# A routing step moved by one chunk, mixed rows copied by DMA and turned in one pass, and two zero products fewer

## The chip, the cores and the metric

The kernel runs on one core of one Trainium2 chip. The metric is the time of one execution on the device, in microseconds. The engines are named as the profile names them: PE is TensorE (PEld its weight loads), DVE is VectorE, ACT is ScalarE, POOL is GpSimd, and SP is SyncE, which here only issues DMAs.

## What is computed

Three layers stand behind one another, all in float32 at the interface.

1. Attention with a window of 64 keys: 4 batches, 8 heads, 576 positions, 64 per head.
2. A mixture of experts over the 2304 rows of 512 that come out. Each row goes to the two of 8 experts whose noisy logits are highest, and the two results are added with softmax weights:

```python
noisy_logits = x @ w_gate + np.log1p(np.exp(x @ w_noise)) * noise
top2 = np.argpartition(-noisy_logits, 2, axis=1)[:, :2]
h = np.maximum(x[mask] @ w1[e], 0.0)
out[mask] += top2_w[mask, k, None] * (h @ w2[e])
```

3. A dense layer of 2048 hidden values with a gate that is quadratic between -1 and 1:

```python
h = x @ w_in
g = np.where(h >= 1, h, np.where(h <= -1, 0.0, (h + 1) ** 2 / 4))
out = g @ w_out
```

## The kernel before

**Attention and routing.** `step(u)` runs the attention of 18 tiles of 128 rows, two steps per tile. Ahead of it PE works through zero products (`warm(9)`, L662), whose result nobody uses, and then forms the first scores (`A`, L347). Beside the attention the rows' logits are formed (`Gm`), and the generator `route(g)` (L490) turns the logits of a group of tiles into expert numbers and positions; there are three groups, of 8, 4 and 6 tiles. A generator is taken on by one or more of its `yield`s each time `advance` (L636) is called. For the last group the order in which it does so is: the gate's logarithm on DVE and ACT; the noise; the two largest with their indices (L529 to L533); the one-hot sum `ohs` (L543) and counts; the position products on PE (L558 to L564), which read `ohs`; the positions on DVE (L567 to L581). After that `mark_r` and `mark_e` make one-hot marks on DVE and ACT, and `place` (L628) multiplies them on PE, so that lists of row numbers per expert come out.

The last group is not finished when the attention ends. `tail` (L796) takes it on, and `more()` (L1278) takes `tail` on by one call. In the loop over `seq` (L1288) the first unit, `ui == 0`, has eight chunks; in each, `more()` is called before the next chunk's first product (L1307) and after it (L1349), and for chunk 0 once more after its second product (L1365).

**Experts.** A unit is a set of up to 704 gathered rows of one expert. A chunk is 128 of its hidden values: `mm1` (L877, L891) makes the first product, ACT applies ReLU and writes a rounded high part (L899), DVE writes the rest (L902), and `mm2` (L948, L964) adds up the second product. All products are three single-pass products of high and low parts (type `fp32r`). Iteration `s` of the loop issues `mm1` of chunk `s + 1`, then `mm2` of chunk `s`. Every engine works through its instructions in the order in which the program issues them, and waits for others by semaphores. Between the products, weights of the next unit are split into high and low parts (`split_w`, `split_out`). Results are scattered by POOL's indirect DMAs to `y_dram`, which holds for every row its two experts' results.

**Dense groups.** The last layer runs over five groups of 2, 4, 4, 4 and 4 blocks of 128 rows. For each block:

- `prep_gather` (L1015) loads the two results of its rows, `y1` and `y2`, into the scratch pool `sc` (for the second group's blocks 0 to 2 into one tile of `raw`). SP issues these loads, for the second group POOL.
- The mix `w1*y1 + w2*y2` is made in one of two ways. `prep_mix` (L1039; first group and groups three to five) scales both on ACT and adds them on POOL. `mix_two` (L1032; second group) scales `y1` on ACT and does the rest on DVE in one operation (L1036).
- The mixed block is turned by four transposes against an identity: `xpose` (L751, L759) for the first group, `xturn` (L1230, L1236) for the others. Rows that were gathered for the experts have type `F32R` and are turned against `idr`; mixed rows are float32 and are turned against `idn`.
- ACT copies the turned block out of the bank (L762, or `xcopy`, L1242).

For the first group, block `b` is loaded in chunk `3 + b` of the last expert unit, mixed at the head of the next chunk (before that chunk's `mm1`), and turned ahead of `mm2` of the chunk after that. For the second group, `FILL` (L1402) says in which first product of the first group a block is mixed, and `TURN` and `COPY` (L1397) at which pair of chunks and which seventh `(p, j)` it is turned and copied. Groups three to five are loaded, mixed and turned in pairs 0 to 3 of the group before (L1437 to L1446). From the second group on the first product is a seven-product scheme on half blocks (`wino`, L1178), with the gate on ACT and DVE (L1196 to L1206).

Of the kernel before, what the change touches and what calls it, by code (L numbers as in the profile page):

```python
# [11 lines left out]
F32 = mybir.dt.float32  # L12
F32R = mybir.dt.float32r
# [4 lines left out]
AF = mybir.ActivationFunctionType  # L18
ALU = mybir.AluOpType
AX = mybir.AxisListType  # L20

P = 128
B, H, S, D = 4, 8, 576, 64
N = B * S
DM = H * D
# [32 lines left out]
def fused_kernel(ctx, tc, qT, kT, v, wg, noise, wcat, out, wd=None):  # L58
# [595 lines left out]
    def warm(n, to=OB[:, 1, :]):  # L654
        for _ in range(n):
            nc.tensor.matmul(to, lhsT=wz[:, 0:P], rhs=wz, start=True, stop=True)
# [2 lines left out]
        nc.tensor.matmul(IDS[:, 0:2 * NK], lhsT=wz[:, 0:P], rhs=wz[:, 0:2 * NK], start=True, stop=False)  # L659

    open_ids()
    warm(9)  # L662
    A(0)
    for u in range(2):
        top(u)
# [68 lines left out]
            gat["0a", b] = t  # L734


    xT = {}
    WD, WX = NB * P, CAPS[0]
    TR = bank[7]
# [11 lines left out]
    def xpose(key, b, m=P, TR=TR):  # L751
        if key not in xT:
            xT[key] = x_tiles(key, F32R)
        hi, lo = xT[key]
        t = gat.pop((key, b))

        o, i = (TR.bitcast(F32R), idr) if t.dtype == F32R else (TR, idn)
        for k in range(4):
            nc.tensor.transpose(o[:, k * P:k * P + m], t[0:m, k * P:k * P + P], i[0:m, 0:m])  # L759
        tv = TR.rearrange("p (k t) -> p k t", k=4)[:, :, 0:m]  # L760
        sl = slice(b * P, b * P + m)
        nc.scalar.activation(hi[:, :, sl], tv, AF.Copy)  # L762
        nc.vector.tensor_tensor(out=lo[:, :, sl], in0=tv, in1=hi[:, :, sl].bitcast(F32), op=ALU.subtract)
# [267 lines left out]

    def mix_two(un, b):  # L1032
        (y1, y2), t = gat[un["key"], b]
        nc.scalar.activation(y1, y1, AF.Copy, scale=wts[:, t, 0:1])
        yield
        nc.vector.scalar_tensor_tensor(out=y2, in0=y2, scalar=wts[:, t, 1:2], in1=y1, op0=ALU.mult, op1=ALU.add)  # L1036
        gat[un["key"], b] = y2

    def prep_mix(un, b):  # L1039
        if un["e"] is None:  # L1040
            y, t = gat[un["key"], b]
            y1, y2 = y
            nc.scalar.activation(y1, y1, AF.Copy, scale=wts[:, t, 0:1])
            nc.scalar.activation(y2, y2, AF.Copy, scale=wts[:, t, 1:2])  # L1044
            nc.gpsimd.tensor_tensor(out=y2, in0=y2, in1=y1, op=ALU.add)  # L1045
            gat[un["key"], b] = y2

    def prep_xpose(un, b, tr=TR):
        xpose(un["key"], b, n_rows(un, b), tr)
# [180 lines left out]
    def xturn(ui, b):  # L1230
        un = units[ui]
        t = gat.pop((un["key"], b))
        free = [bank[7]] + [x for x in bank[2:7] if x not in units[ui - 1]["m2"]]
        held[ui, b] = to = free[b % len(free)]
        for k in range(4):
            nc.tensor.transpose(to[:, k * P:k * P + P], t[:, k * P:k * P + P], idn)  # L1236

    def xcopy(ui, b):
        if b == 0:
# [38 lines left out]
    def more(k=1):  # L1278
        for _ in range(k):
            next(rest, None)  # L1280
# [7 lines left out]
    for s in range(len(seq)):  # L1288
# [15 lines left out]
            dec_load(ndl)  # L1304
            ndl += 1
        if ui == 0:
            more()  # L1307
        if s == NF:
            choice_weights()
        if ui == U7A - 1 and f == 2:  # L1310
# [22 lines left out]
                    prep_xpose(x, b, bank[0] if ui == WIDE else bank[4] if ui == WIDE - 1 and b == NB else TR)  # L1333
        for x, b, w in ahead:
            if f == w + 1 and x["e"] is None:
                fill.append(lambda x=x, b=b: prep_mix(x, b))
        while fill:
            fill.popleft()()

        while ndone < min(s + 2, len(seq)):  # L1340
            do_mm1(ndone)
            ndone += 1
        if decode and ndec < n64:
            dec_a(ndec)
        if s == len(seq) - 1:
# [15 lines left out]
        do_mm2(s, ahead_xpose)  # L1361
        if s in (0, 2):
            rest_w(EW - 2 + s // 2, slice(0, 1024))
        if s == 0:
            more()  # L1365
        for _ in range(SPLITS[ui][f] if ui in SPLITS else int(0 < ui < U7A)):

            if nsplit == SP:
# [20 lines left out]
        if ui == U7B and f:  # L1389
# [4 lines left out]

    AT = ({(4, 0): (None,), (4, 4): (0,), (4, 5): (1,), (5, 0): (2,), (5, 1): (3,), (5, 3): (4,), (6, 2): (5,), (6, 3): (6,)},
          {})
    TURN, COPY = {(3, 0): (0,), (3, 1): (1,), (3, 6): (2,), (4, 0): (3,)}, {(3, 3): (0, 1), (4, 2): (2, 3)}  # L1397
    g1 = FIRST2 + 1

    def later(fn, *a):  # L1400
# [9 lines left out]
    for q, (ui, p) in enumerate(items):  # L1410
# [22 lines left out]
        for j in range(7):  # L1433
            if nxt:
                late = ui == FIRST2
                if late:
                    if p == 0 and j < 4:  # L1437
                        prep_gather(nxt, j)
                elif p < 2 and j in (0, 1):
                    prep_gather(nxt, 2 * p + j)  # L1440
                if not late:
                    if 1 <= p < 3 and j in (2, 4):
                        prep_mix(nxt, 2 * (p - 1) + j // 2 - 1)
                    if 2 <= p < 4 and j in (1, 3):
                        xturn(ui + 1, 2 * (p - 2) + j // 2)
                        xcopy(ui + 1, 2 * (p - 2) + j // 2)  # L1446
                else:
                    for b in TURN.get((p, j), ()):
                        xturn(ui + 1, b)
                    for b in COPY.get((p, j), ()):  # L1450
                        xcopy(ui + 1, b)
                    if p == 4 and j > 4:
                        xsums(ui + 1, (0, 1) if j == 5 else (2, 3))
                for x in AT[late].get((p, j), ()):
                    xsums(ui + 1) if x is None else xsplit(ui + 1, x)
            if j < len(g):
                g[j]()
            if gen:
                next(gen)
                if q == NPR - 2:  # L1460
                    close_gate()
            for x in ms[len(ms) * j // 7:len(ms) * (j + 1) // 7]:
                x()
# [33 lines left out]
```

## Time and profile before

| | us |
|---|---|
| median of 3 runs | 954.12 |
| lowest and highest | 953.84, 954.31 |
| the profiled execution | 953.95 |
| its span, first to last instruction | 952.2 |

| engine | busy us | share of the span |
|---|---|---|
| PEld | 832.8 | 87% |
| DVE | 659.5 | 69% |
| ACT | 444.3 | 47% |
| POOL | 222.1 | 23% |

Times in the profile's rows count from the span's start. An instruction of a timeline is shown with its start, its length, its engine, its line, what it writes and reads, and how many like it were merged. A bracket gives how long the engine stood idle before it and what ended that. A matmul's length holds its latency, so that matmuls that follow each other overlap; the step from one start to the next says what one costs.

### The profile page before, as it was taken

How to read it: one execution, taken by the hardware profiler on the slowest of the kernel's cores; microseconds unless marked ns; L12 is line 12 of the kernel's file. 1: busy time of each engine (PE TensorE's matmuls, PEld its weight loads, DVE VectorE, ACT ScalarE, POOL GpSimd, SP SyncE). 2: the span in 40 equal slices, each digit the busy share in tenths (PEclk: the TensorE clock that was granted, in tenths of full speed). 3: DMA queues.
4: the chain of work that ended last, by engine and by line, in shares of the span. 5: the costliest groups of instructions: out<-in, count | busy, mean ns of one | idle time of the engine just before them, and what ended most of it. 6: DMA issues, size and time to landing. Idle time of an engine off the chain costs nothing. (4 is left out here: it accounts for less than half of the span.)

```text
span 952.2 us, 18037 instructions
## 1 busy us (share of the span) xinstructions
PE 938.4 (99%) x6779; PEld 832.8 (87%) x6781; DVE 659.5 (69%) x1386; ACT 444.3 (47%) x920; POOL 222.1 (23%) x273
## 2 busy tenths in 40 slices
PE   9999899999999999999999999999999999999998
PEld 6887788988889889889888889988998899899997
DVE  5688665477997968889543377766766777677664
ACT  7897325345565555555432366343334334442221
POOL 4222013133544353354402030013002201300000
PEclk9999999999999999999999999999999999999999
DMA  8884126555888777767626567775586458556521
GB/s 269 289 271 150 50 89 195 187 194 198 285 287 285 256 233 278 258 211 250 244 89 202 201 212 254 256 235 175 177 273 208 149 173 306 174 176 207 188 94 44
DMA packets 91274, 196.95 MB, mean 207 GB/s; under 512 B 7320, under 2 KB 18072, under 8 KB 91184
## 3 DMA queue, kind: packets, MB, share of 16 engines
q1 hardware_dynamic: 83152, 171.68, 54.4%
q0 software_dynamic: 6736, 21.86, 6.4%
q10 hardware_dynamic: 1296, 2.23, 0.6%
q8 instruction: 54, 0.88, 0.4%
q14 instruction: 36, 0.29, 0.1%
HBM read 155.45 MB, written 40.29 MB: 206 GB/s over the span
## 5 line engine op out<-in xcount | busy, mean ns | idle before, releaser
L964 PE MATMUL bank<-wo,hall 128*128 128x512 f32 x864 | 237.6, 394 | 0.0
L964 PE MATMUL bank<-w,hall 128*128 128x512 f32 (+3 forms) x944 | 236.2, 398 | 0.1
L964 PEld LDWEIGHTS bank<-w,hall 128*128 128x128 f32 (+3 forms) x944 | 168.8, 185 | 35.5 <-issue 0.3
L964 PEld LDWEIGHTS bank<-wo,hall 128*128 128x128 f32 x864 | 146.7, 188 | 17.4 <-DVE hall L910 0.2
L899 ACT ACTIVATE hall<-bank 128x288 fp32r<-128x288 f32 (+6 forms) x128 | 54.0, 422 | 219.7 <-PE bank L891 197.3
L891 PE MATMUL bank<-xhie,w 128*128 128x288 f32 (+4 forms) x768 | 122.6, 302 | 0.5 <-DVE hall L902 0.4
L891 PEld LDWEIGHTS bank<-xhie,w 128*128 128x128 f32 x768 | 113.5, 188 | 7.5 <-DVE hall L902 1.3
L902 DVE SCALAR_TENSOR_TENSOR hall<-bank,hall 128x288 fp32r<-128x288 f32 (+7 forms) x168 | 59.9, 390 | 84.3 <-ACT hall L899 76.2
L149 DVE TENSOR_TENSOR w<-raw,w 128x1024 fp32r<-128x1024 f32 (+1 forms) x69 | 82.0, 1188 | 23.7 <-ACT w L158 19.4
L1178 PEld LDWEIGHTS bank<-xb,wi 128*128 128x128 f32 x576 | 80.5, 188 | 10.1 <-DVE cg L1168 1.2
L1202 ACT ACTIVATE hall<-cg 128x512 fp32r<-128x512 f32 x64 | 40.3, 629 | 100.5 <-DVE cg L1200 100.5
L1178 PE MATMUL bank<-xb,wi 128*128 128x256 f32 x576 | 84.7, 282 | 0.6 <-DVE cg L1168 0.3
L1178 PEld LDWEIGHTS bank<-xc,wi 128*128 128x128 f32 x480 | 67.2, 188 | 7.6 <-DVE wg L1163 0.6
L1178 PE MATMUL bank<-xc,wi 128*128 128x256 f32 x480 | 70.2, 281 | 0.2 <-DVE wg L1163 0.2
L1045 POOL TENSOR_TENSOR y<-y,y 128x512 f32<-128x512 f32 x14 | 19.1, 1365 | 217.1 <-ACT y L1044 217.1
L158 ACT ACTIVATE w<-raw 128x1024 fp32r<-128x1024 f32 (+1 forms) x71 | 69.4, 977 | 0.0
L891 PE MATMUL bank<-xloe,w 128*128 128x288 f32 (+4 forms) x384 | 69.1, 302 | 0.0
L204 POOL TENSOR_TENSOR td<-rawd 128x512 f32<-128x512 f32 x32 | 33.3, 1040 | 139.7 <-DVE rawd L202 111.8
L1196 ACT ACTIVATE mg<-cg 128x512 f32<-128x512 f32 x64 | 40.1, 626 | 46.8 <-DVE cg L1168 45.1
L1197 DVE SCALAR_TENSOR_TENSOR cg<-mg,cg 128x512 f32<-128x512 f32 x64 | 46.9, 733 | 18.8 <-ACT mg L1196 18.8
L891 PEld LDWEIGHTS bank<-xloe,w 128*128 128x128 f32 x384 | 58.0, 188 | 0.0
L1206 DVE SCALAR_TENSOR_TENSOR hall<-cg,hall 128x512 fp32r<-128x512 f32 x64 | 45.9, 717 | 9.1 <-ACT hall L1202 8.7
(284 smaller groups left out, 1442.8 us busy)
## 6 DMA issues: line engine op xcount, KB each, us to landing
wi<-w1o SPq DMA_DIRECT2D x56, 1024.0 KB
raw<-wcat SPq DMA_DIRECT2D x64, 512.0 KB
rawd<-wd SPq DMA_DIRECT2D x32, 512.0 KB
w1o<-so SPq DMA_DIRECT2D x64, 256.0 KB
y<-y_dram SPq DMA_DIRECT2D x28, 256.0 KB
vE<-v SPq DMA_DIRECT2D x18, 260.0 KB
x_dram<-x SPq DMA_DIRECT2D x18, 256.0 KB
k<-kT SPq DMA_DIRECT2D x8, 512.0 KB
```

Of the source, the lines that this page charges most:

```text
L149: nc.vector.tensor_tensor(out=w[:, 1, c], in0=t[:, c], in1=w[:, 0, c].bitcast(F32), op=ALU.subtract)
L158: nc.scalar.activation(w[:, 0, c], t[:, c], AF.Copy)
L204: nc.gpsimd.tensor_tensor(out=t, in0=hf, in1=lf, op=ALU.add)
L891: nc.tensor.matmul(ps, lhsT=l[k], rhs=r[:, k, s:s + w], start=(c == 0), stop=(c == len(prods) - 1))
L899: nc.scalar.activation(hh, ps, AF.Relu)
L902: nc.vector.scalar_tensor_tensor(out=t, in0=ps[:, c], scalar=0.0, in1=hh[:, c].bitcast(F32), op0=ALU.max, op1=ALU.subtract)
L964: nc.tensor.matmul(M2[b][0:w], lhsT=h2[:, o:o + w], rhs=r[n], start=(first and a == 0), stop=(last and a == end))
L1178: nc.tensor.matmul(ps, lhsT=w[:, l, k * P:k * P + P], rhs=r[:, m, k, :], start=(c == 0), stop=(c == len(prods) - 1))
L1196: nc.scalar.activation(st["m"], c, AF.Relu, scale=0.5)
L1197: nc.vector.scalar_tensor_tensor(out=c, in0=st["m"], scalar=1.0, in1=c, op0=ALU.min, op1=ALU.subtract)
L1202: nc.scalar.activation(h2[:, 0:T], c, AF.Copy, scale=-1.0)
L1206: nc.vector.scalar_tensor_tensor(out=h2[:, T:2 * T], in0=c, scalar=-1.0, in1=h2[:, 0:T].bitcast(F32), op0=ALU.mult, op1=ALU.subtract)
```

## The change

- `warm(9)` becomes `warm(7)`.
- The additional call of `more()` after chunk 0's second product is gone; the third chunk's first call (`s == 2`, before its `mm1`) takes `tail` on by two calls.
- All mixes are made by `mix_two`, which now scales `y2` on ACT and adds `w1*y1` on DVE. A DMA issued by POOL then copies the mixed rows from `y2` to `y1`, or, for blocks 0 to 2 of the second group, to a new tile of `sc`. `prep_mix` is gone. For the first group the scaling stands where the mix stood, and the DVE operation and the copy behind the next `mm1`. In groups three to five the scaling stands at sevenths 2 and 4, DVE's operation and the copy at 3 and 5.
- All turns go through `turned`, which reads the rows as `F32R` and uses `idr`.
- The second group's blocks 2 and 3 are turned at (4, 0) and (4, 1) instead of (3, 6) and (4, 0).

```diff
-    warm(9)
+    warm(7)
...
+    def turned(to, t, k, m=P):
+        nc.tensor.transpose(to.bitcast(F32R)[:, k * P:k * P + m], t if t.dtype == F32R else t.bitcast(F32R), idr[0:m, 0:m])
...
-        o, i = (TR.bitcast(F32R), idr) if t.dtype == F32R else (TR, idn)
         for k in range(4):
-            nc.tensor.transpose(o[:, k * P:k * P + m], t[0:m, k * P:k * P + P], i[0:m, 0:m])
+            turned(TR, t[0:m, k * P:k * P + P], k, m)
...
     def mix_two(un, b):
         (y1, y2), t = gat[un["key"], b]
-        nc.scalar.activation(y1, y1, AF.Copy, scale=wts[:, t, 0:1])
+        nc.scalar.activation(y2, y2, AF.Copy, scale=wts[:, t, 1:2])
         yield
-        nc.vector.scalar_tensor_tensor(out=y2, in0=y2, scalar=wts[:, t, 1:2], in1=y1, op0=ALU.mult, op1=ALU.add)
-        gat[un["key"], b] = y2
-
-    def prep_mix(un, b):
...
+        nc.vector.scalar_tensor_tensor(out=y2, in0=y1, scalar=wts[:, t, 0:1], in1=y2, op0=ALU.mult, op1=ALU.add)
+        if un is units[FIRST2 + 1] and b < 3:
+            y1 = pool["sc"].tile([P, DM], F32, tag="s", name=f"yr{t}")
+        nc.gpsimd.dma_start(out=y1, in_=y2)
+        gat[un["key"], b] = y1
...
         for k in range(4):
-            nc.tensor.transpose(to[:, k * P:k * P + P], t[:, k * P:k * P + P], idn)
+            turned(to, t[:, k * P:k * P + P], k)
...
         if ui == 0:
-            more()
+            more(1 + (s == 2))
...
             if f == w + 1 and x["e"] is None:
-                fill.append(lambda x=x, b=b: prep_mix(x, b))
-        while fill:
-            fill.popleft()()
+                fill.append(mix_two(x, b))
+                next(fill[-1])
 
         while ndone < min(s + 2, len(seq)):
             do_mm1(ndone)
             ndone += 1
+        while fill:
+            next(fill.popleft(), None)
...
-        if s == 0:
-            more()
...
-    TURN, COPY = {(3, 0): (0,), (3, 1): (1,), (3, 6): (2,), (4, 0): (3,)}, {(3, 3): (0, 1), (4, 2): (2, 3)}
+    TURN, COPY = {(3, 0): (0,), (3, 1): (1,), (4, 0): (2,), (4, 1): (3,)}, {(3, 3): (0, 1), (4, 2): (2, 3)}
...
                     if 1 <= p < 3 and j in (2, 4):
-                        prep_mix(nxt, 2 * (p - 1) + j // 2 - 1)
+                        fill.append(mix_two(nxt, 2 * (p - 1) + j // 2 - 1))
+                        next(fill[-1])
+                    if 1 <= p < 3 and j in (3, 5):
+                        next(fill.popleft(), None)
```

## Rows read from the trace of the kernel before

**Rows 1.** The page: busy time, share of the span and instructions of each engine.
```profile
PE 938.4 (99%) x6779; PEld 832.8 (87%) x6781; DVE 659.5 (69%) x1386; ACT 444.3 (47%) x920; POOL 222.1 (23%) x273
```

**Rows 2.** One line's view, L1236: xcount, shortest/median/longest ns, first and last start.
```profile
L1236 PE MATMUL bank<-idn,y x64: 270/272/275, 579.1 to 825.1; 128*128 128x128 f32 x64
```

**Rows 3.** Timeline of PE: start us, us, engine line op out<-in xcount [idle before <-releaser].
```profile
471.97 0.46 PE L759 MATMUL bank<-idr,xg7a 128*128 128x128 f32 x4
...
472.26 2.08 PE L964 MATMUL bank<-w,hall 128*128 128x512 f32 x8
...
579.78 0.60 PE L1236 MATMUL bank<-idn,y 128*128 128x128 f32 x4
...
580.13 2.31 PE L964 MATMUL bank<-wo,hall 128*128 128x512 f32 x9
```

**Rows 4.** Timeline at the start of the kernel.
```profile
1.47 3.69 PE L656 MATMUL ob<-wz 128*128 128x512 bf16 x9
...
11.16 0.40 PE L355 MATMUL bank<-mask,id 64*64 64x512 bf16 x2 [0.85 <-ACT p L380]
```

**Rows 5.** Timeline of the first unit, beside which the last routing group runs.
```profile
111.42 0.50 DVE L530 MAX8 mx<-ny 128x8 f32<-128x8 f32 x6
...
113.53 0.18 PE L558 MATMUL bank<-ohs,tri 128*128 128x48 bf16 x1 [1.89 <-DVE ohs L543]
...
113.70 3.89 PE L964 MATMUL bank<-w,hall 128*128 128x512 f32 x9
...
113.87 0.55 DVE L902 SCALAR_TENSOR_TENSOR hall<-bank,hall 128x384 fp32r<-128x384 f32 x1
...
117.44 1.55 PE L891 MATMUL bank<-xhi0a,w 128*128 128x384 f32 x8
...
117.73 0.26 DVE L593 TENSOR_SCALAR ohe<-io,rf 128x145 f16<-128x145 f16 x1
...
119.88 2.33 PE L964 MATMUL bank<-w,hall 128*128 128x512 f32 x9
```

**Rows 6.** Windows: stretch, us, busy time of PE, PEld, DVE, ACT, POOL, granted clock, DMA.
```profile
11.20:20.00 8.80, 8.80 (x178) 7.69 (x181) 5.06 (x12) 8.04 (x25) 2.44 (x7) 1.00 0.89 293
...
113.90:117.30 3.40, 3.40 (x9) 2.63 (x9) 3.30 (x13) 0.57 (x2) 0.00 (x0) 0.50 0.00 0
```

**Rows 7.** Timeline where the first dense group's block 0 is mixed and turned.
```profile
545.82 0.72 ACT L1043 ACTIVATE y<-y,wts 128x512 f32<-128x512 f32 x1 [2.48 <-DMA y<-y_dram]
...
547.52 0.52 DVE L902 SCALAR_TENSOR_TENSOR hall<-bank,hall 128x256 fp32r<-128x256 f32 x2 [2.92 <-ACT hall L899]
...
548.47 1.23 DVE L1127 TENSOR_TENSOR wo<-wr,wo 128x1024 fp32r<-128x1024 f32 x1 [0.43 <-ACT wo L1126]
...
548.63 0.66 PE L759 MATMUL bank<-idn,y 128*128 128x128 f32 x4
```

**Rows 8.** Timeline where the second dense group's blocks are mixed and turned.
```profile
576.12 0.75 DVE L1036 SCALAR_TENSOR_TENSOR y<-y,wts 128x512 f32<-128x512 f32 x1 [1.87 <-ACT y L1034]
...
577.92 0.75 DVE L1036 SCALAR_TENSOR_TENSOR y<-y,wts 128x512 f32<-128x512 f32 x1
...
579.11 0.60 PE L1236 MATMUL bank<-idn,y 128*128 128x128 f32 x4
...
579.90 0.72 ACT L1034 ACTIVATE y<-y,wts 128x512 f32<-128x512 f32 x1 [0.36 <-DMA y<-y_dram]
```

**Rows 9.** Windows: a pair of chunks of a later group.
```profile
624.32:634.87 10.55, 10.55 (x68) 9.50 (x67) 7.41 (x14) 5.14 (x9) 2.67 (x2) 1.00 0.81 280
```

**Rows 10.** Timeline of transfers and of VectorE beside POOL's issues.
```profile
568.02 2.24 POOL L1023 DMA_DIRECT2D y<-y_dram  x3 [4.74 <-DMA y_dram<-y7b,rank_i]
...
568.25 0.43 DVE L922 SCALAR_TENSOR_TENSOR r<-m,r 128x256 f32<-128x256 f32 x1
...
623.73 1.23 SPq L1029 DMA_DIRECT2D y<-y_dram  x2
...
626.09 0.71 ACT L1043 ACTIVATE y<-y,wts 128x512 f32<-128x512 f32 x1
```

More of the change, by code (lines that the diff above doesn't have):

```diff
@@ L1033, in mix_two @@
         (y1, y2), t = gat[un["key"], b]
-        nc.scalar.activation(y1, y1, AF.Copy, scale=wts[:, t, 0:1])
+        nc.scalar.activation(y2, y2, AF.Copy, scale=wts[:, t, 1:2])
         yield
-        nc.vector.scalar_tensor_tensor(out=y2, in0=y2, scalar=wts[:, t, 1:2], in1=y1, op0=ALU.mult, op1=ALU.add)
-        gat[un["key"], b] = y2
-    def prep_mix(un, b):
[L1040 to L1046, printed above, removed]
+        nc.vector.scalar_tensor_tensor(out=y2, in0=y1, scalar=wts[:, t, 0:1], in1=y2, op0=ALU.mult, op1=ALU.add)
[3 more added lines that the diff above has]
+        gat[un["key"], b] = y1
     def prep_xpose(un, b, tr=TR):
```

## The prediction

> **What bounds the kernel.** I read the page first. TensorE (PE) is busy for nearly the whole span [rows 1], so every microsecond has to be looked for in PE's own order: what PE does less of, and where it will stand still. The line's own view gives the number of transposes that change [rows 2]; the PE timeline gives what one costs, because there the start of the next instruction can be read [rows 3]. Then I went to the three places that the diff touches: the start [rows 4], the routing beside the first unit [rows 5, 6], and the two dense groups at which mixed rows are turned soon after they are mixed [rows 7, 8].
>
> **Cheaper transposes: -1.1 us.** Four single-pass transposes hold PE from 471.97 to 472.26, 0.29 us; four of the present kind from 579.78 to 580.13, 0.35 us [rows 3]. The step is taken from a group's own start to the next line's, since the matmul's mean also holds its latency. There are 64 in L1236 [rows 2] and 8 for the two blocks of the first dense group, 18 blocks of four; 18 x 0.06 = 1.1 us, all of it on PE's path.
>
> **Two zero products fewer: -0.1 us.** Nine of them take 3.69 us [rows 4], 0.41 each, so 0.8 us is the most that can go. But the score products behind them need q and k, and the next score tile is held for 0.85 us by ScalarE's exponentials [rows 4]: most of what PE saves turns into that wait. Bounds 0 and -0.8; near 0, since ScalarE and not PE ends that wait.
>
> **Routing's call one chunk later: -1.9 us.** Now PE ends the third chunk's first product at 111.64, stands for 1.89 us on VectorE's one-hot sum (L543), and only then may start nine second products [rows 5]. Behind the wait those nine run at clock 0.50 [rows 6] and take 3.89 us where the next nine take 2.33 [rows 5]: 1.56 us more. Upper bound of the gain: 1.89 + 1.56 = 3.4 us. After the change the nine products stand ahead of the position products and start at 111.64; they end about 113.7. L902 (0.55 us, at 113.87) now precedes the one-hot sum on VectorE, which is ready about 114.0, so 0.3 to 0.5 us of wait stay. Then come twelve first products (eight take 1.55 us [rows 5], so about 2.1), to 116.3. The next thing PE needs are marks that VectorE ends at 117.73 + 0.26 = 117.99 [rows 5]; VectorE works without a gap from 111.42 to there, on the same instructions in another order, so that time does not move. The nine products that now start at 119.88 start at about 118.1: 1.8 us, and 0.1 more from the shorter waits of the rounds behind it. What is late next is VectorE's marks. The lower bound is 0.4 us, if that new wait of up to 1.6 us brings the clock down as the old one did.
>
> **The mix.** Per block POOL loses an addition, ScalarE one of two scalings; VectorE gains one operation of 0.75 us (the same form as L1036 [rows 8]) and POOL a DMA issue. In a later group a pair of chunks with two mixes takes 10.55 us, all of it PE's, with VectorE busy for 7.41 and POOL for 2.67 [rows 9]: 1.5 us more of VectorE still fit, and the copy has a whole pair before it is turned. Cost nothing, covered by PE's products; bound 0.2 us either way for each of three groups. Three further tiles of the scratch pool and the two turns put off to the fifth pair also cost nothing while ScalarE's copy at (4,2) finds them done.
>
> **A wait for the copy, first dense group: +2.7 us.** Here a block is turned in the chunk after its mix. ScalarE waits for the load until 545.82, the two scalings end by 547.2, VectorE's L902 pair runs to 548.04 [rows 7]. The new VectorE operation stands behind that pair: 548.8. Only then may POOL issue the copy (behind it in POOL's order stand the last unit's scatters, which are not due before the unit ends), and the transposes stand at the head of PE's order at 548.63 [rows 7], with eight second products behind them that nothing else holds. No row shows an on-chip copy. Nearest below: two loads of the same 256 KB, issued from 623.73, of which ScalarE uses one at 626.09, so 2.4 us at most [rows 10]. Nearest above: POOL sits for 4.74 us until its last scatter has landed [rows 10]. I take 2.6, near the lower end, as this copy has no load of POOL's ahead of it: landing 551.4, a wait of 2.7 us; bounds 2.2 and 4.9. The group's second block does not wait: its copy goes out while PE still works off the first wait.
>
> **The second dense group: +2.1 us.** VectorE mixes block 0 by 576.87 and block 1 by 578.67; PE turns them at 579.11 and 579.78 [rows 8]. With 2.6 us the copies land at 579.5 and 581.3, and PE loses 1.5 us. But the group's loads go through the same POOL queue and the last of them is waited for until 579.90 [rows 8]; behind it the copies land about 581.0 and 581.9: 2.1 us, in two pieces of 1.9 and 0.2 with a product between. Bounds 1.5 and 3.0. Blocks 2 and 3 are turned in the next pair, late enough.
>
> **The clock: +1.5 us.** A wait of 1.89 us was followed by a stretch at 0.50 that cost 1.56 [rows 5, 6]; one of 0.85 was not [rows 4, 6]. The first new wait is longer than 1.89, the second comes in pieces not longer than that: I count one such stretch, 1.5 us; bounds none and two.
>
> **POOL's issue.** VectorE's next operation after the mix is a weight split of 1.23 us [rows 7]. If POOL could not issue beside it, the first copy would land 1.2 us later and the sum would be 958.5. But POOL issued three loads in 2.24 us, an even 0.75 each, while VectorE's L922 ran, which also reads two tiles [rows 10]; I take no such wait. The Trainium skill's page SBUF — State Buffer, section SBUF: two separate sides, says that a DMA issued by POOL gets no descriptors written while VectorE, in its two-port modes, holds the port pair that both share. That would be the higher of the two sums; the row does not show it.
>
> **Sum.** The profiled execution took 953.95 us (span 952.2), 0.17 under the median of 954.12. 953.95 - 1.1 - 0.1 - 1.9 + 2.7 + 2.1 + 1.5 = 957.15; with 0.17, 957.3. About 0.2% (1.9 us) is what a measurement of this kernel tells from no change.
>
> **Rivals.**
> - Both waits bring the clock down: 957.3 + 1.5 = 958.8. For it: the first piece in the second group is as long as the wait that did so. Chance 0.24.
> - Neither does: 955.8, still no difference that can be told. Chance 0.12.
> - The other side, the copy is in time. It decides at 548.63 and 579.11: if the mix is earlier or the copy under a microsecond, only the gains are left, 953.95 + 0.17 - 3.1 = 951.0. For it: in the second group VectorE is done 2.2 and 1.1 us ahead of the turn, and the 2.4 us of a load is only a top for what lies below. Against: VectorE cannot mix before 548.04 [rows 7], so even a copy of 0 us would wait 0.2. Chance 0.16.
> - Only the first group waits, at full clock: 951.0 + 2.7 = 953.7. Chance 0.05.
> - The routing call does not do what it says: the wait goes from L558 to the marks and the clock falls there too. 957.3 + 1.5 = 958.8. For it: 116.3 to 118.1 is nearly as long as 1.89. Against: it is broken by the position products, each started as its mark comes. Chance 0.04.
> - VectorE holds up POOL's issue, as weighed above: 957.3 + 1.2 = 958.5. Chance 0.04, as the row speaks against it. The page named there is what it would follow.
>
> **Numbers.** The forecast, both waits and one slow stretch, has 0.35; its own range is 956.2 to 958.6. Faster: 0.16. Within 0.2%, 952.2 to 956.0: 0.12 + 0.05 = 0.17. Slower: 0.35 + 0.24 + 0.04 + 0.04 = 0.67. The range leaves out the case of copies in time and takes in the others with the bounds of the copy: 953.5 to 960.2.
>
> **What would show it.** Transposes of mixed rows with a step of 0.29 instead of 0.35 us for four; no wait of 1.9 us before L558 and no half clock at 114 to 117; the position products waiting for VectorE's marks near 118. Near 546 to 549 (2 us earlier than now) PE should stand for over 2 us before the first turn of a mixed block, released by the copy's DMA, again at the third group of plain products, each perhaps followed by 0.50 in the clock's row. No such wait at both places would make the prediction wrong, and so would PE waiting on VectorE in the later groups.

## The result: 961.64 us, slower, and the profile after

The changed kernel takes 961.64 us (median of 6 runs, 959.24 to 962.80) against 954.00 us (6 runs, 953.82 to 954.31) for the kernel before: the ratio is 1.0078 (95% interval 1.0065 to 1.0091). The direction is the one forecast; the time lies 4.3 us above the forecast and 1.4 us above the range. The profiled execution is the shortest of the six: 959.24 us, span 957.5, mean granted clock 0.996. In the other five the mean granted clock is 0.993 to 0.995.

To see where the time went I cut both spans at the same five instructions of PE. Each number is the distance from one such start to the next, in us; the rest of the span behind the last mark is 4.3 to 4.4 everywhere.

| stage, up to | before | after | difference |
|---|---|---|---|
| the first unit's first product (start, attention) | 103.00 | 103.60 | +0.60 |
| the second unit's first product (first unit, routing) | 63.49 | 61.37 | -2.12 |
| the first turn of a mixed block (experts) | 382.14 | 384.80 | +2.66 |
| the second group's first product (first dense group) | 48.99 | 54.12 | +5.13 |
| the last second product (groups two to five) | 350.25 | 349.24 | -1.01 |

The routing gains what was forecast and the later groups gain about what their transposes should. The two dense groups at which a turn follows its copy closely lose 7.8 us.

The page of the changed kernel: busy time, and the chain of work that ended last (share of the span by engine and line; a wait for a transfer stands in it as `DMA`). The chain's line is cut off by the view:

```profile
PE 939.9 (98%) x6779; PEld 833.1 (87%) x6779; DVE 665.1 (69%) x1400; ACT 436.6 (46%) x906; POOL 213.7 (22%) x277
...
PE bank L966 21%; PE bank L1174 16%; PE bank L893 2%; DMA y<-y_dram 1%; PE bank L738 1%; DMA yr<-y 1%; DVE cg L1196 0%; DVE hall L1202 0%; DMA y<-y 0%; ACT hall L1198 0%; ACT xf L1238 0%; ACT mg L1192 0%; DVE y L1038 0%; DVE cg L1164 0%; DV
```

PE is busy 1.5 us longer than in [rows 1], although its transposes became cheaper and two products are gone. In the fourth row of the table alone it is busy 2.9 us longer (51.88 against 48.99), at a mean clock of 0.94 instead of 1.00: that is work at half the clock. The copies stand in the chain by name, `y<-y` (first group) and `yr<-y` (second group).

The timeline of the changed kernel where the first dense group's blocks are mixed (DVE L1038), copied (POOL L1041) and turned (PE L738); it answers to [rows 7]:

```profile
545.95 0.69 PE L893 MATMUL bank<-xlo7a,w 128*128 128x288 f32 x4
549.77 0.71 PE L738 MATMUL bank<-idr,y 128*128 128x128 f32 x4 [3.13 <-DMA y<-y]
550.28 3.47 PE L966 MATMUL bank<-w,hall 128*128 128x512 f32 x8
...
545.87 0.74 DVE L1038 SCALAR_TENSOR_TENSOR y<-y,wts,y 128x512 f32<-128x512 f32 x1
546.53 1.22 DVE L1123 TENSOR_TENSOR wo<-wr,wo 128x1024 fp32r<-128x1024 f32 x1
...
549.07 0.74 DVE L1038 SCALAR_TENSOR_TENSOR y<-y,wts,y 128x512 f32<-128x512 f32 x1
...
547.21 0.59 POOL L1041 DMA_DIRECT2D y<-y  x1 [16.55 <-PE bank L893]
550.36 0.57 POOL L1041 DMA_DIRECT2D y<-y  x1 [2.56 <-DVE y L1038]
```

PE stands for 3.13 us on the copy. DVE is done at 546.61, POOL issues at 547.21, and the turn starts 2.56 us after that. The eight second products behind the turn then take 3.47 us.

The same three steps at the second dense group, with POOL's loads (L1025) and the mix's scaling on ACT (L1036); it answers to [rows 8]:

```profile
577.28 0.75 DVE L1038 SCALAR_TENSOR_TENSOR y<-y,wts 128x512 f32<-128x512 f32 x1 [0.48 <-ACT y L1036]
...
582.52 0.72 ACT L1036 ACTIVATE y<-y,wts 128x512 f32<-128x512 f32 x1 [0.47 <-DMA y<-y_dram]
...
569.56 2.24 POOL L1025 DMA_DIRECT2D y<-y_dram  x3 [3.75 <-DMA y_dram<-y7b,rank_i]
...
578.33 0.54 POOL L1041 DMA_DIRECT2D yr<-y  x1 [5.40 <-DVE y L1038]
...
584.07 0.75 PE L738 MATMUL bank<-idr,yr 128*128 128x128 f32 x4 [2.24 <-DMA yr<-y]
584.61 0.76 PE L966 MATMUL bank<-wo,hall 128*128 128x512 f32 x1
585.29 0.75 PE L738 MATMUL bank<-idr,yr 128*128 128x128 f32 x4
585.84 3.51 PE L966 MATMUL bank<-wo,hall 128*128 128x512 f32 x11
```

This copy needs 5.74 us from issue to turn, more than twice the first group's. The loads that POOL issued from 569.56 are still landing: ACT waits for the last until 582.52. Between the two turns PE's weight load waits another 0.43 us for the second copy.

Windows of the changed kernel (columns as in [rows 6]; the last three are granted clock, DMA share and GB/s):

```profile
547.00:549.80 2.80, 0.03 (x1) 0.03 (x1) 1.92 (x4) 1.02 (x2) 0.59 (x1) 1.00 0.51 158
549.90:553.30 3.40, 3.40 (x11) 2.55 (x12) 1.90 (x2) 1.54 (x2) 0.57 (x1) 0.50 0.44 170
577.00:584.00 7.00, 4.83 (x33) 4.28 (x31) 5.17 (x11) 4.95 (x13) 1.48 (x3) 1.00 1.04 385
584.00:587.40 3.40, 3.33 (x13) 2.62 (x14) 1.12 (x4) 1.32 (x3) 0.68 (x2) 0.50 1.01 367
114.00:117.40 3.40, 2.97 (x22) 2.38 (x20) 3.19 (x14) 0.20 (x1) 0.00 (x0) 1.00 0.00 0
```

Two things are to be seen. The clock is 0.50 (1.2 GHz) behind each of the two waits, and 1.00 behind the routing, where it was 0.50 [rows 6]. And the DMA engines are half idle while the first group's copy is under way (0.51): they carry no packet from 547.2 to 548.2, and then, until 549.2, this copy alone. While the second group's copies are under way they are full (1.04). What fills them is, by the view of the queues from 578.3 to 584.1 (packets, MB, share of the 16 engines; `q0` is POOL's queue with the loads and the copies, `q1` SP's, here with weights):

```profile
q1 hardware_dynamic: 629, 1.19, 58.8%
q0 software_dynamic: 307, 0.99, 44.6%
```

The timeline of PE beside the last routing group, which answers to [rows 5]:

```profile
112.07 2.25 PE L966 MATMUL bank<-w,hall 128*128 128x512 f32 x9
114.45 0.18 PE L558 MATMUL bank<-ohs,tri 128*128 128x48 bf16 x1
...
117.67 0.67 PE L634 MATMUL bank<-ohe,ohr 128*128 128x145 f16 x3 [0.57 <-DVE ohr L586]
...
118.53 2.31 PE L966 MATMUL bank<-w,hall 128*128 128x512 f32 x9
```

The wait of 1.89 us before L558 is gone, and the next thing late is, as forecast, DVE's marks, with 0.57 us at its longest.

### The profile page after: what moved, and what is told of

Read it like the earlier page. It is cut to its first block, busy times and chain, and to the rows that moved or that the text cites. A ratio compares the mean times of both kernels' runs of the same rounds, so it can differ in the third digit from the quotient of the medians.

```text
span 957.5 us, 18068 instructions
## 1 busy us (share of the span) xinstructions
PE 939.9 (98%) x6779; PEld 833.1 (87%) x6779; DVE 665.1 (69%) x1400; ACT 436.6 (46%) x906; POOL 213.7 (22%) x277
## 5 line engine op out<-in xcount | busy, mean ns | idle before, releaser
L1041 POOL DMA_DIRECT2D y<-y x15 | 8.2, 547 | 224.8 <-PE bank L1174 117.9
```

## The experiments

The eleven runs were timed in three sets, each beside the kernel before, whose median differs from set to set (951.87 for the first four runs, 953.76 for the next four, 952.26 for the last three; the last two sets on one chip). So kernels of different sets are compared by ratio, and a tenth of a per cent between sets tells nothing. The stages of the table above, in us, for every profiled execution (a: start and attention, b: first unit, c: to the first turn of a mixed block, d: first dense group, e: the rest):

| kernel | a | b | c | d | e | span |
|---|---|---|---|---|---|---|
| routing call alone | 102.30 | 60.79 | 381.60 | 49.04 | 350.24 | 948.3 |
| seven zero products alone | 103.06 | 61.20 | 381.68 | 49.00 | 350.22 | 949.5 |
| copy and turns alone | 103.47 | 62.75 | 384.86 | 54.45 | 349.70 | 959.6 |
| after, nine zero products | 105.58 | 60.80 | 384.85 | 54.28 | 349.74 | 959.6 |
| after without the copy | 103.45 | 61.04 | 381.65 | 48.99 | 350.23 | 949.7 |
| copy issued by SP | 102.81 | 61.79 | 384.08 | 49.99 | 349.18 | 952.1 |
| more room | 103.67 | 61.41 | 381.74 | 53.05 | 349.23 | 953.5 |
| products through the waits | 102.85 | 61.76 | 384.85 | 51.76 | 350.39 | 956.0 |
| copies where there is room | 102.98 | 60.83 | 381.85 | 49.93 | 349.92 | 949.9 |
| routing call alone, again | 103.10 | 60.78 | 381.70 | 48.98 | 350.24 | 949.2 |
| after, again | 103.13 | 60.81 | 384.95 | 56.22 | 349.39 | 958.9 |

### One part alone: routing

```diff
 # against the kernel before
-            more()
+            more(1 + (s == 2))
...
-        if s == 0:
-            more()
```

> Kernel before with the routing call moved alone. If the wait of 1.89 us before L558 and the slow stretch behind it go and only a wait on the marks of some 0.8 us stays, the time falls by 1.9 to 2.1 us, to about 952.0. Rival: the new wait on the marks brings the clock down in part of the runs, then 952.0 to 953.5 with a spread of 1.5 us.

Measured: 950.61 us against 951.87, ratio 0.9991 (0.9982 to 1.0001). Run a second time beside other kernels:

> The kernel before with the routing call moved alone, a second time, beside the version above on one chip. Theory: the kernel before -0.4 us where its execution has no stretch at half clock after the call, -2.0 us where it has one; by the mean of both -0.4 to -1.5 us here, and 0.7 us above the version with copies where there is room. Rival: no difference from either.

Measured: 951.09 us against 952.26, ratio 0.9984 (0.9971 to 0.9997). Stage b is 60.8 us in both, 2.7 under the 63.49 of the kernel before as first profiled, whose stretch ran at half clock, and only 0.4 under the 61.20 of an execution with the old routing and no such stretch (the next kernel). So the gain is 0.4 us of wait plus the price of a slow stretch where there is one; by the ratios it comes to 0.9 us and 1.5 us. The first interval includes no change and the second ends near it, so the gain is small, and its size is not settled.

### One part alone: the zero products

```diff
 # against the kernel before
-    warm(9)
+    warm(7)
```

> Kernel before with seven zero products instead of nine. Theory: the clock rises about 2.5 us later, because PE waits for q and k between the first scores, and the first score tile ends 0.6 us later: 954.6, and as the slow stretch at 114 us and what follows may move with it, a spread of over 1 us. Rival (as predicted): nothing or 0.1 us less, 953.9.

Measured: 951.59 us against 951.87, ratio 1.0001 (0.9991 to 1.0010). Nothing can be told. Stage a takes from 102.30 to 105.58 us in the kernels with nine products and from 102.81 to 103.67 in those with seven: the start varies by more than the edit. What differs at the start does not follow the edit: with seven products the first 32 score products (L364) take 1.85 us here at a clock of 0.50, but 1.04 at 1.00 in the kernel whose copy is issued by SP; with nine they take 1.04 at 1.00 in the kernel before, but 1.62 in the changed kernel with nine. The forecast did not see this. Nor does the wait for ScalarE's exponentials take up what PE saves: it is 0.85 us with nine products [rows 4] and 0.85 with seven.

This execution also has the old wait, and not what followed it in [rows 6]:

```profile
113.57 0.18 PE L558 MATMUL bank<-ohs,tri 128*128 128x48 bf16 x1 [1.89 <-DVE ohs L543]
...
113.75 2.31 PE L964 MATMUL bank<-w,hall 128*128 128x512 f32 x9
...
113.60:117.00 3.40, 3.40 (x23) 3.02 (x23) 3.26 (x13) 0.22 (x1) 0.00 (x0) 1.00 0.00 0
```

The same wait of 1.89 us, and a clock of 1.00 behind it. A wait of that length may bring the clock down and may not; what decides it no run here shows.

### One part alone: copy and turns

The routing call and the nine zero products as before; all the rest of the change in.

```diff
 # against the changed kernel
-    warm(7)
+    warm(9)
...
-            more(1 + (s == 2))
+            more()
...
+        if s == 0:
+            more()
```

> Mix, copy, single-pass turns and the put-off turns alone; nine zero products, routing as before. Theory: two waits of PE of 3.1 and 2.2 to 2.7 us on the copy, a slow stretch of 1.5 us behind each, 2 us back from cheaper transposes and less work beside the later groups: 954.0 + 7 = 961. Rival: the waits bring down the clock only in some runs, then 958 to 961 with a spread of up to 3 us.

Measured: 960.83 us against 951.87, ratio 1.0089 (1.0074 to 1.0104): +8.5 us. Stages c and d carry it, with waits of 3.08 and 2.46 us and both slow stretches. This kernel also has the old wait of 1.89 us before L558, and here 0.50 follows it again (114.60 to 118.00). The line's own view gives how long 18 copies took from issue to landing:

```profile
DMA to landing us min/median/max: 2.3/4.4/7.0
```

### The changed kernel with nine zero products

```diff
 # against the changed kernel
-    warm(7)
+    warm(9)
```

> Changed kernel with nine zero products again. Theory: 0.6 us less than the changed kernel's 961.6 and, if the late rise of the clock is what makes its runs differ by 3.6 us, a spread of under 1 us near 958.6. Rival: the spread comes from the waits on the copies, then it stays at 3 us and the median is 961.0.

Measured: 960.24 us against 951.87, ratio 1.0086 (1.0071 to 1.0101), no different from the copy alone. Neither the theory's 958.6 nor the rival's spread of 3 us came: the four executions lie between 960.08 and 961.33. The waits are 3.08 and 2.31 us. The windows show what became of the clock behind the first and the second:

```profile
551.30:554.70 3.40, 3.40 (x21) 2.92 (x22) 1.92 (x2) 1.55 (x2) 0.56 (x1) 1.00 0.52 193
583.90:590.70 6.80, 6.41 (x20) 5.10 (x21) 1.06 (x3) 1.20 (x2) 0.92 (x2) 0.50 0.71 251
```

Here the longer wait was followed by no slow stretch, and the shorter one by a stretch of 6.8 us.

### The change without the copy

The mixed rows stay in `y2` and are turned from there as plain fp32.

```diff
 # against the changed kernel
-        nc.tensor.transpose(to.bitcast(F32R)[:, k * P:k * P + m], t if t.dtype == F32R else t.bitcast(F32R), idr[0:m, 0:m])
+        o, i = (to.bitcast(F32R), idr) if t.dtype == F32R else (to, idn)
+        nc.tensor.transpose(o[:, k * P:k * P + m], t, i[0:m, 0:m])
...
-        nc.gpsimd.dma_start(out=y1, in_=y2)
-        gat[un["key"], b] = y1
+        gat[un["key"], b] = y2
```

> The changed kernel without the copying DMA: the mixed rows stay in y2 and are turned from there as plain fp32; seven zero products and the moved routing call stay. Theory (the copy and what it brings at the first and the second dense group make the whole slowdown): the two waits for the copy (3.13 us and 2.24 + 0.43 us) and the two stretches of 3.4 us at half the granted clock go, the turns cost 0.06 us more for each of about 18 blocks, and the time is between 2 us below the kernel before and 0.5 us above it. Rival (the later clock rise at the start, or the order around the moved routing call, carries part of the loss): 1 us or more above the kernel before.

Measured: 951.89 us against 953.76, ratio 0.9984 (0.9975 to 0.9992), -1.5 us: inside what the theory gave and well away from the rival. The timeline of PE at the first dense group:

```profile
546.14 0.66 PE L739 MATMUL bank<-idn,y 128*128 128x128 f32 x4
546.55 2.08 PE L967 MATMUL bank<-w,hall 128*128 128x512 f32 x8
```

No wait over 0.1 us, and eight products in 2.08 us that took 3.47 behind the wait. This is the price of one slow stretch there, 1.39 us. In stages c and d the copy costs (384.80 - 381.65) + (54.12 - 48.99) = 8.3 us of the changed kernel's profiled execution; in e it gives 1.0 back.

### The copy issued by SP

```diff
 # against the changed kernel
-        nc.gpsimd.dma_start(out=y1, in_=y2)
+        nc.sync.dma_start(out=y1, in_=y2)
```

> The changed kernel with the copy issued by SP in place of POOL. Theory (POOL's issue and POOL's queue, with the loads of the second group's rows ahead, lengthen the copies): the second group's waits fall from 2.24 + 0.43 us to between 0 and 1.3 us in all, since the copies no longer stand behind those loads, and the first group's wait of 3.13 us falls by up to 0.6 us; one slow stretch stays at the first group, the second goes if its wait is under 1 us: the changed kernel -1 to -4 us. Rival (the copy itself, or the traffic of the DMA engines whichever queue issues it, takes the time): the waits stay within 0.4 us and the time is that of the changed kernel; or the copies stand behind SP's weight loads and the waits grow.

Measured: 955.27 us against 953.76, ratio 1.0021 (1.0008 to 1.0034). The timeline, first and second dense group (SPq is SP's queue of instructions; a row of x2 starts with its first):

```profile
546.33 0.52 SPq L1041 DMA_DIRECT2D y<-y  x1
...
548.68 0.54 PE L738 MATMUL bank<-idr,y 128*128 128x128 f32 x4 [2.35 <-DMA y<-y]
...
575.16 3.86 SPq L1041 DMA_DIRECT2D yr<-y  x2
...
580.31 0.53 PE L738 MATMUL bank<-idr,yr 128*128 128x128 f32 x4 [1.11 <-DMA yr<-y]
```

Both waits are shorter, by 0.78 and by 1.56 us (1.11 for 2.24 + 0.43). SP issues 0.03 us after the mix, POOL 0.60 us after it in the first group and 0.30 in the second. But the second group's first copy still takes 580.31 - 575.16 = 5.15 us, on a queue without POOL's loads: the queue explains the smaller part, and the theory's reason is only half right. The queues' view shows the larger part, in the stretches 575.2:576.8, 578.4:579.2 and 579.2:579.6 (`q0` POOL's loads, `q1` SP's queue):

```profile
q0 software_dynamic: 176, 0.59, 97.3%
q1 hardware_dynamic: 8, 0.01, 3.1%
...
q0 software_dynamic: 5, 0.02, 5.2%
...
q1 hardware_dynamic: 5, 0.01, 6.7%
```

The loads have the DMA engines almost alone until 576.8. Most of the copy moves from there to 578.4 (131 packets). Then 5.2%, about one engine of the 16, is still at the loads until 579.2, the others stand idle, and only behind them come the last packets of SP's queue ahead of the next copy's, by their place the rest of this copy. So the loads delay the copy on another queue too. A run without them was not made; and in the changed kernel SP's weights fill the engines besides. The Trainium skill's page DMA: Bandwidth & Descriptors, section Queues, rings and completion order, says that each DMA engine serves in turn the queues that have work for it; the rows agree in so far as a queue of its own did not get the copy past the loads (5.15 us), but the turns themselves they do not show.

Behind neither wait is there a stretch at 0.50 in this profile, so the time fell by some 6 us against the changed kernel's ratio, more than the 1 to 4 us expected. Its ten executions range from 952.4 to 957.5 us, with mean clocks from 1.000 to 0.996.

### More room between copy and turn

```diff
 # against the changed kernel
-Y0, LOOK = 3, 1
+Y0, LOOK = 2, 1
...
-                if f == (turn_at[b] if ui == WIDE - 1 else w + 2):
+                if f == (turn_at[b] if ui == WIDE - 1 else w + 2 + (ui == U7B)):
...
-    TURN, COPY = {(3, 0): (0,), (3, 1): (1,), (4, 0): (2,), (4, 1): (3,)}, {(3, 3): (0, 1), (4, 2): (2, 3)}
+    TURN, COPY = {(3, 5): (0,), (3, 6): (1,), (4, 0): (2,), (4, 1): (3,)}, {(3, 6): (0, 1), (4, 2): (2, 3)}
```

> The changed kernel with more room between the copy and its turn: the first dense group is mixed after the second position and turned one position later; the second group's first two blocks are turned two to five weight tiles later. Theory (only the missing room costs; copy and single-pass turn are otherwise cheaper): the first group's wait goes (0.2 us or less), the second group's falls to 0.8 us or less, neither stretch at half clock is seen, and the time is the changed kernel -6 to -8.5 us, so about the kernel before or up to 1.5 us below. Rival (the copies slow the transfers of weights or of the next group's rows, or hold POOL): waits appear at other places and the time stays 2 us or more above the kernel before.

Measured: 952.72 us against 953.76, ratio 0.9992 (0.9982 to 1.0003): 0.9% under the changed kernel's ratio, about 8 us, as the theory gave. The timeline of PE, first turn of the first group, then first and third of the second:

```profile
546.82 0.53 PE L738 MATMUL bank<-idr,y 128*128 128x128 f32 x4
...
579.93 0.54 PE L738 MATMUL bank<-idr,yr 128*128 128x128 f32 x4 [0.61 <-DMA yr<-y]
...
586.30 0.54 PE L738 MATMUL bank<-idr,yr 128*128 128x128 f32 x4 [1.63 <-DMA yr<-y]
```

The first group's wait is gone. In the second group 0.61 us stay, and with the first blocks no longer late the third block's copy is: issued at 579.24, it needs 7 us, and PE waits 1.63. In this execution, one of the longer of twelve (955.19), a slow stretch follows.

### Work instead of the wait

Products that nobody uses, 30 ahead of the first group's block 0 and 24 and 5 ahead of the second group's blocks 0 and 1, keep PE working until the copy has landed. They are added work.

```diff
 # against the changed kernel
+    def busy(to, n):
+        for _ in range(n):
+            nc.tensor.matmul(to[:, 0:P], lhsT=idr, rhs=idr, start=True, stop=True)
...
+        if key == "g0" and b == 0:
+            busy(TR, 30)
...
+        if ui == FIRST2 + 1 and b < 2:
+            busy(to, (24, 5)[b])
```

> The changed kernel with products nobody uses ahead of the three turns that wait (30 ahead of the first dense group's first block, 24 and 5 ahead of the second group's first two), so that TensorE works through the waits. Theory (TensorE's idling in the waits lowers its clock after them, worth about 1.5 us for each stretch): the waits' length stays as time, the stretches at 0.50 go, and the time is the changed kernel -2 to -3.5 us. Rival (the clock falls for another reason, or the products hold the turns up): within 1 us of the changed kernel or slower.

Measured: 958.36 us against 953.76, ratio 1.0060 (1.0036 to 1.0084). The timeline of PE at the first group, and the windows behind both groups' first turns:

```profile
546.16 3.46 PE L742 MATMUL bank<-idr 128*128 128x128 f32 x30
549.46 0.52 PE L738 MATMUL bank<-idr,y 128*128 128x128 f32 x4
549.82 2.07 PE L972 MATMUL bank<-w,hall 128*128 128x512 f32 x8
...
549.50:552.90 3.40, 3.40 (x23) 2.94 (x22) 1.92 (x2) 1.55 (x2) 0.56 (x1) 1.00 0.49 187
...
583.50:586.90 3.40, 3.40 (x21) 2.93 (x21) 0.00 (x0) 0.62 (x2) 0.00 (x0) 1.00 0.77 270
```

The time until the turn is the same (stage c 384.85), the clock stays at 1.00, and the eight products take 2.07 us. Stage d falls by 2.4 us against the changed kernel's first profile. The ratio lies 0.2% (1.7 to 2.5 us) under the changed kernel's in its three measurements with seven or nine zero products, at the lower end of what the theory gave, but the intervals overlap (1.0036 to 1.0084 here). The mean clocks say more: three of the four executions have 0.999 to 1.000, where 13 of the 14 executions of those three measurements have 0.993 to 0.996 and one has 0.998. So the copies by themselves do not bring the clock down, and PE's standing still in the waits is the likely cause of the slow stretches. It is not shown for every execution: the fourth is still long (962.41, mean clock 0.994), and its trace was not taken.

### Copies only where there is room, and the changed kernel again

The routing call moved, nine zero products, and copy with single-pass turn only in groups three to five.

```diff
 # against the changed kernel
-    warm(7)
+    warm(9)
...
+        if un in (units[FIRST2], units[FIRST2 + 1]):
+            gat[un["key"], b] = y2
+            return
...
-            turned(to, t[:, k * P:k * P + P], k)
+            turned(to, t[:, k * P:k * P + P], k, one=ui > FIRST2 + 1)
```

> The kernel with the routing call moved, nine zero products, and copy plus single-pass turn only in the later dense groups (12 blocks); the first and the second group's blocks are turned from the mixed rows as plain fp32, as before. Theory (a copy costs only where its turn follows closely, and the single-pass turn gives 0.06 us a block): no waits and no stretch at half clock, 12 x 0.06 = 0.7 us below the kernel with the routing call alone, and the kernel before -1 to -3 us. Rival (the later copies disturb transfers or are late now and then): as the kernel with the routing call alone, or above it.

Measured: 950.85 us against 952.26, ratio 0.9986 (0.9977 to 0.9995). That is below the kernel before, but not to be told from the routing call alone on the same chip (951.09). Stage e gains 0.3 us rather than 0.7, with a wait of 0.23 us for one late copy in it; stage d holds a wait of 0.69 us behind a load that landed late (ScalarE stood 2.21 us for it). The expected 0.7 us did not show in the time.

> The changed kernel unaltered, a second time, for its spread beside the others. Theory (two waits of about 5.8 us together, and stretches at half clock that follow them in some executions and not in others): the same two waits within 0.3 us; none, one or two stretches at 0.50 in the profiled execution, and a spread of several us between executions with the granted clock lower in the longer ones. Rival (the loss is the same in every execution): both stretches there, spread under 1.5 us.

Measured: 960.39 us against 952.26, ratio 1.0084 (1.0068 to 1.0099), four executions from 958.38 (mean clock 0.998) to 960.60 (0.994). The profiled one has waits of 3.16 and 3.27 us, and these windows:

```profile
548.10:554.90 6.80, 6.01 (x21) 4.97 (x21) 2.52 (x3) 1.54 (x2) 0.56 (x1) 0.50 0.52 175
585.60:589.00 3.40, 3.40 (x14) 2.79 (x13) 0.00 (x0) 1.19 (x2) 0.00 (x0) 0.51 0.80 284
```

That is 10.2 us at 0.50, in place of 6.8 in the first profile; 0.8 us of it lie still inside the first wait, which ends at 548.89. Within the changed kernel the longer executions are those with the lower mean clock, as the theory said.

## Why the prediction went wrong in size

**The clock was the step that failed.** It was put as "I count one such stretch, 1.5 us; bounds none and two". Its price was right: 1.39 us by the same eight products in the changed kernel and without the copy. Its number was not. The profiled execution has two stretches; the repeated one has 6.8 + 3.4 us at 0.50, the kernel with nine zero products 6.8 behind a single wait. A stretch of 3.4 us at 0.50 lowers the mean clock of 957 us by 3.4 x 0.5 / 957 = 0.0018. The five other executions have 0.994 in the mean where the profiled one has 0.996, so they stand for about one stretch more, 1.4 us. That is about half of the 2.4 us between the profiled execution and the median, and a rough estimate: those five have no trace, and the means are rounded to 0.001. The other half stays open; the start alone differs by up to 3.3 us between executions (102.30 to 105.58 in column a). The premise was a rule of lengths read from one execution: 1.89 us brings the clock down, 0.85 does not. The runs contradict it: 1.89, 2.35 and 3.08 us without a slow stretch, 1.63 with one. The bound "two" also took one wait to cause one stretch at most.

**The range.** Its upper end, 960.2, is the sum for one stretch with both copies at their upper bounds (957.15 + 2.2 + 0.9). With the same bounds, the rival with two stretches, to which the prediction gave 0.24, reaches 958.8 + 2.2 + 0.9 = 961.9. The median of 961.64 lies inside that and outside the range as stated.

**First dense group, +2.7 forecast, 3.1 measured.** The copy took 2.56 us where 2.6 was taken. What was missing is POOL's start, 0.60 us after the mix, which the sum put at nothing; 0.2 of it came back, as the mix ended with PE's last product (546.61 and 546.64) and not 0.2 us after it.

**Second dense group, +2.1 forecast, 2.24 + 0.43 measured.** Within its bounds of 1.5 to 3.0, in part by luck: the copy took 5.74 us from issue to turn, not the 4.1 us from the mix's end (576.87) to the landing (581.0) that the forecast allowed. DVE was done 3.8 us before PE came to the turn (578.03 and 581.83), where the kernel before had it done 2.2 us ahead, and this hid most of the error. What the forecast had right is that the copies land behind the loads: it put them 1.1 us behind the last one (579.90 and 581.0), and 1.5 us were measured (582.52 and 584.07). SP's weights, which then fill the DMA engines, were in no term.

**Transposes, -1.1 forecast.** Four take 0.29 us where they took 0.35:

```profile
729.01 0.46 PE L738 MATMUL bank<-idr,y 128*128 128x128 f32 x4
729.30 0.92 PE L1174 MATMUL bank<-xc,wi 128*128 128x256 f32 x6
```

In stage e, where 12 x 0.06 = 0.7 was due, the kernels with copies gain 0.5 to 1.1 us, except where a copy is late: with products through the waits one costs 0.82 us before 727.41 and the stage gains nothing. So "the copy has a whole pair before it is turned" does not always hide it. What the mix's new shares of DVE and POOL cost was rightly put at nothing: no wait on DVE's mix stands in PE's rows of the later groups.

**Routing, -1.9 forecast, -2.1 in the profiles, -0.9 and -1.5 by the ratios of the routing call alone.** The mechanism was right, with DVE's marks next at 117.67 and nine products at 118.53 (forecast 118.1). But most of it was the slow stretch of the execution that I had been shown: nine products in 3.89 us [rows 5] that take 2.31 behind the same wait in the kernel with seven zero products alone. Without that stretch 0.4 us are left, the lower bound that the prediction gave for another reason.

**Zero products, -0.1 forecast, nothing to be told measured.** The reason given, that the wait for ScalarE's exponentials takes up the saving, is not what happens: that wait stays at 0.85 us. What was missing is the start's own variation, 102.3 to 105.6 us to the first unit; it belongs in the range of a sum made against one execution.

**POOL's issue, nothing forecast.** POOL issued beside VectorE's two-input operation, at 547.21 while L1123 ran from 546.53 to 547.75, and the copy landed 2.56 us later, against 2.35 from SP. POOL's start was 0.55 us behind the mix also where DVE then stood idle (mix done 549.81, issue 550.36). In the changed kernel's second profile the copy issued beside L1123 took 2.5 us to land, and the next one, issued beside an idle DVE, 2.3. The rival by which DVE holds the issue up by 1.2 us does not hold here. The trap that the Trainium skill's page SBUF — State Buffer describes in its section SBUF: two separate sides is one of VectorE's two-port modes; no row here tells the mode in which L1123 ran, so the trap is not seen, but not tested either.

The profiled execution is 2.1 us above the forecast's own sum (959.24 - 957.15), and the steps account for it: second stretch +1.3 (2.8 for 1.5; 54.12 - 48.99 - 2.67 of waits, plus 6 x 0.06 for cheaper transposes, leaves 2.8 for the two), first wait +0.4, second +0.6, start +0.7 (+0.6 for -0.1), routing -0.2, transposes -0.3, and -0.5 in the experts, where the kernel before had lost 0.5 us (382.14 in stage c, 381.6 to 381.9 in all five kernels without an early copy): +2.0.

Of the rivals, the one with both waits bringing the clock down (958.8, chance 0.24) is the one that came; its time lies 0.4 us under the profiled execution, but 2.8 us under the median. The copy in time (951.0) comes true only with more room made for it.

## What to carry to other kernels

A transfer put between two engines of a tight chain costs its whole latency wherever the consumer follows closely, and that latency is the one under the traffic of that place: here 2.3 to 2.6 us where it had the DMA engines to itself, 5 to 7 us beside the second group's loads and weights. Price a wait on TensorE as its length plus 1.4 us for each slow stretch behind it, and take the number of stretches as uncertain, since two executions of one kernel differ in it. Before a saving of 0.06 us a block is bought with a copy, see at which blocks the copy is off the path, and what is late next once the first wait is gone.

## What was not expected of the hardware

- The same wait is followed by half clock in one execution and not in another: 1.89 us before L558 with 0.50 behind it [rows 6] and with 1.00; 3.1 us before the first turn with 3.4 us at 0.50, with 6.8, and with none.
- An on-chip copy of 256 KB took 2.3 us at the least and 7.0 at the most, with a median of 4.4 over 18 of one kernel.
- SP issued a DMA 0.03 us after its releaser, POOL 0.30 to 0.60 us after it.
- A copy issued on SP's queue, 575.16, waited for loads on POOL's: those had 97.3% of the DMA engines' time from 575.2 to 576.8, and the turn that waited for the copy started 5.15 us after its issue.
